# Where the first unit's low parts stand on VectorE: ahead of the folds of the phase that ends, or behind them

## The chip, the cores and the metric

The kernel runs on one core of a Trainium2 chip. The metric is the time of one execution on the device in microseconds (us), lower is better. Engines are named as the profile names them: PE is TensorE's matmul, PEld its weight load, DVE is VectorE, ACT is ScalarE, POOL is GpSimd, SP is SyncE.

## The reference

Three layers follow one another over 4 x 4096 tokens of 192 channels in float32: a causal convolution over 7 taps whose weights are a softmax for each of 8 heads, a gated layer of width 1536, and a squared-relu layer of width 2048.

```python
w = softmax(weight)                                  # [8 heads, 7 taps]
x = sum over k of w[head(c), k] * x_pad[b, s + k, c]  # 16384 x 192
gate = 1.0 / (1.0 + np.exp(-(x @ w_gate)))
x = (gate * (x @ w_val)) @ w_out                     # 192 -> 1536 -> 192
r = np.maximum(x @ w_in, 0.0)
out = (r * r) @ w_out2                               # 192 -> 2048 -> 192
```

## The kernel before

**High and low parts.** TensorE multiplies float32 in a format with fewer bits (fp32r). Every operand is therefore split into a high part (the value rounded to fp32r, written by ACT) and a low part (the value minus its high part, written by DVE), and a product is the sum of three: high x high, low x high and high x low. For the hidden activations the tiles are called `s` (the float32 value, 3 buffers), `gh` (high, 5 buffers) and `gl` (low, 5 buffers), each of 128 x 512.

**Phases and units.** The 16384 tokens are cut into 32 tiles of 512. A *phase* is one tile through one layer: kind 1 is the gated layer, kind 2 the squared-relu layer. The order is five phases of kind 1, then kind 1 and kind 2 in turn (27 of each), then the last five of kind 2: 64 phases, with 63 places where one ends and the next starts. A phase of kind 1 has 12 *units* of 128 hidden columns (one hidden tile each), a phase of kind 2 has 8 units of 256 (two hidden tiles each).

**A unit's steps.** `rows(u)` (L492) issues 18 matmuls on the PE that make the unit's two PSUM banks (`pg` and `pv`, or `ph` twice). `activate(u)` reads them: sigmoid or relu on ACT (L505), a product on DVE (`times`, L509), the high part on ACT (`high`, L514). `low` (L519) is the subtraction on DVE. `cols(u)` (L557) issues 10 matmuls for each hidden tile, which add into four PSUM banks (accA and accB, for each half of the rows). Its first two matmuls read `gh`, its next two `gl`. All these matmuls come in pairs on the two halves of 64 rows, and the two of a pair start together.

**The order of the work.** It is written out by hand; every engine works through its own queue in that order. In the main loop unit k of a phase (k from 0) does: rows(u), activate(u), then `cols` of units that are waiting, then `side[e]` (work put in by hand: a tap of the convolution, a step of the conversion of weights, a step of the preparation of the next operand), then low(u). At k = 0 both units left over from the phase that ends get their `cols`, at k = 1 none, from k = 2 on one: so the PE's order at a start is rows(u0), cols of two old units, rows(u1), rows(u2), cols(u0). When the last `cols` of a phase is issued, `fold` follows at once: ACT copies one half of the sums (L572, L576), DVE adds the other half (L573, L577), and a join (ACT L580, DVE L581) brings 64 channels together. The fold gives the four banks back; cols(u0) takes them again. In what follows u0, u1, u2 are the first three units of the phase that starts.

Of the kernel before, what the change touches and what calls it, by code (L numbers as in the profile page):

```python
# [25 lines left out]
def kernel(  # L26
# [30 lines left out]
    NU1, NU2 = F1 // P, F2 // (2 * P)  # L57
# [422 lines left out]
    def rows(u):  # L480

        xs = (x1 if u.kind == 1 else x2)[u.t]
        u.banks = [banks.take(nm) for nm in (("pg", "pv") if u.kind == 1 else ("ph", "ph"))]
        w, lo = (w1[:, u.f, :], N1 + HB) if u.kind == 1 else (weights2(u.f)[0], NR)


        place = (0, 4, 2)
        steps = [(c, o, p) for c in range(C) for o, p in ((0, 0), (0, 1), (lo, 0))]
        for i, (n, o, p) in enumerate(steps):
            for h, half in enumerate(HALVES):  # L490
                c = n ^ h if n < 2 else n
                nc.tensor.matmul(  # L492
                    u.banks[h][1], w[half, o + c * P : o + (c + 1) * P],
                    xs[1][half, place[n] + p, :],
                    start=(i == 0), stop=(i == len(steps) - 1),
                )
        if u.last:
            operands.give(xs)
# [18 lines left out]
    def low(v):  # L517
        v.gl = gp.tile([P, NT], F32R, tag="gl", name="gl", bufs=5)
        nc.vector.tensor_tensor(v.gl, v.s, v.gh.bitcast(F32), op=ALU.subtract)  # L519

    def activate(u):

        acts = []
        for i in range(1 if u.kind == 1 else 2):
            acts.append(act(u, i))
            times(u, acts[-1])
        banks.give(*u.banks)
        u.hidden = [high(s) for s in acts]
# [3 lines left out]
    def cols(u):  # L532

        key = (u.kind, u.t)
        if u.f == 0:
            acc[key] = [[banks.take(f"acc{nm}") for nm in "AB"] for _ in HALVES]
        sums = acc[key]
        order = []  # L540
        for i, v in enumerate(u.hidden):
            if u.kind == 1:
                w, lo = w1[:, u.f, NR:], N1 + HB
            else:
                w, lo = weights2(u.f)[1][:, i, :], NO + HB
            wa, wb, wl = w[:, 0:P], w[:, P : 2 * P], w[:, lo : lo + P]
            first = u.f == 0 and i == 0
            order += [
                (0, wa, v.gh, first), (0, wa, v.gl, False), (0, wl, v.gh, False),
                (1, wb, v.gh, first), (1, wb, v.gl, False),  # L550
            ]
        if u is units[-1]:
            order.sort(key=lambda step: -step[0])
        ends = {step[0]: k for k, step in enumerate(order)} if u.last else {}
        for k, (b, wt, m, first) in enumerate(order):
            for h, half in enumerate(HALVES):
                nc.tensor.matmul(  # L557
                    sums[h][b][1], wt[half], m[half], start=first, stop=ends.get(b) == k,
                )
        return u.last  # L560
# [97 lines left out]
    with tc.manual_schedule():  # L658
# [85 lines left out]
        def convert_and_activate(e, u):  # L744

            one, two = (conv[i] if i < NU1 else None for i in (e + 1, e + 2))
            if two:
                two.word()
            if one:
                one.place()  # L750
                one.follow()
                one.sign()
                if e + 1 + NRAW < NU1:
                    conv[e + 1 + NRAW].load()
            s = act(u, 0)
            if one:
                one.highs()
            if e:
                low(units[e - 1].hidden[0])
            if one:  # L760
                one.power()
                one.lows()
            if two:
                two.middle()
            times(u, s)
            banks.give(*u.banks)
            u.hidden = [high(s)]
            if 1 <= e <= K:
                a1[e]()
            if e == NU1 - 1:  # L770
                low(u.hidden[0])
            if 0 <= e - K - 1 < len(parts1):
                parts1[e - K - 1]()

        for e, u in enumerate(units):
            rows(u)
            if e < NU1:
                convert_and_activate(e, u)
            else:
                activate(u)  # L780
            for o in stores:
                o()
            stores = []
            k = e - max(s for s in starts if s <= e)
            due = len(pending) if k == 0 else 0 if k == 1 else len(pending) - 1
            for _ in range(due):
                v = pending.popleft()
                if cols(v):
                    stores += (evac1 if v.kind == 1 else evac2)(v.t)
            pending.append(u)  # L790
            for o in side[e]:
                o()
            if e >= NU1:
                for v in u.hidden:
                    low(v)
        while pending:
            v = pending.popleft()
# [42 lines left out]
```

## Time and profile before

| | |
|---|---|
| median of 3 runs | 2390.89 us (2389.89 to 2391.37) |
| the profiled execution: its own time | 2391.61 us |
| the profiled execution: span, first to last instruction | 2389.5 us |
| mean granted TensorE clock | 0.997 of full speed |
| busy: PE, DVE, ACT | 99%, 70%, 55% of the span |

The span is what the trace covers; the time of the same execution is 2.1 us longer. A start time in the trace counts from the start of the span. The end of a matmul is modelled and matmuls overlap, so the distance between starts says more on the PE than the busy time does.

### The profile page before, as it was taken

Reading aid. Unit: us, or ns where it says so; the run is one execution under the profiler, and the core shown is the slowest. Engines: PE = TensorE matmul, PEld = TensorE weight load, DVE = VectorE, ACT = ScalarE, POOL = GpSimd, SP = SyncE. Lnnn points to the kernel's source line nnn. Section 1 sums busy time; section 2 is a strip of 40 time slices with the busy share of each in tenths; the row PEclk is TensorE's granted clock in tenths of the full one; section 3 lists DMA queues with packets and bytes.
Section 4 is the critical chain, followed back from the end, with each engine's and each line's share of the span. In section 5 each row is a group of like instructions: output and inputs, shape, how many; then the busy total and the mean of one; then the engine's idle time right before and its main releaser. Section 6 shows DMA issues by size and latency. Waiting matters only on the chain.

```text
span 2389.5 us, 49288 instructions
## 1 busy us (share of the span) xinstructions
PE 2362.3 (99%) x20522; PEld 1930.7 (81%) x20522; DVE 1680.4 (70%) x2677; ACT 1315.6 (55%) x2260; POOL 46.4 (2%) x98
## 2 busy tenths in 40 slices
PE   9999999999999999999999999999999999999998
PEld 5788788888888888888888888888888888888887
DVE  7887867667666767667767677676776766766776
ACT  6556655555555555555555455554555555555665
POOL 1000000000000000000000000000000000000000
PEclk9999999999999999999999999999999999999999
DMA  6222211111112012121011210111111111101111
GB/s 156 58 54 69 51 30 39 38 26 32 30 39 43 21 32 43 25 43 35 20 41 25 43 39 21 37 39 30 39 29 29 38 30 39 34 21 28 40 28 27
DMA packets 226399, 92.12 MB, mean 39 GB/s; under 512 B 202344, under 2 KB 213744, under 8 KB 226176
## 3 DMA queue, kind: packets, MB, share of 16 engines
q1 hardware_dynamic: 224688, 88.19, 17.2%
q8 instruction: 160, 2.62, 0.5%
q0 software_dynamic: 288, 0.59, 0.1%
q14 instruction: 63, 0.52, 0.1%
q10 hardware_dynamic: 1200, 0.20, 0.0%
HBM read 26.03 MB, written 12.58 MB: 16 GB/s over the span
## 4 chain that ended last, share of the span: by engine, by line
PE 78%; issue 16%; DVE 3%; ACT 2%; DMA 1%; SPq 0%; POOLq 0%; DVEq 0%; ACTq 0%; POOL 0%
PE pg L492 28%; PE accA L557 20%; PE ph L492 14%; PE accB L557 13%; PE pv L492 1%; ACT gh L514 1%; DVE s L509 1%; ACT s L505 1%; DVE cvA L390 0%; DVE y L573 0%; DVE gl L519 0%; ACT tb L580 0%; DVE cb L577 0%; ACT ca L572 0%; DVE yb L581 0%
## 5 line engine op out<-in xcount | busy, mean ns | idle before, releaser
L492 PE MATMUL pg<-x,w 64*128 64x512 f32 x3456 | 845.0, 388 | 5.3 <-ACT w L181 3.0
L492 PE MATMUL pv<-x,w 64*128 64x512 f32 x3456 | 844.8, 388 | 0.4 <-DMA x<-x 0.4
L514 ACT CAST gh<-s 128x512 fp32r<-128x512 f32 x896 | 556.9, 623 | 439.1 <-DVE s L509 431.8
L492 PEld LDWEIGHTS pg<-x,w 64*128 64x128 f32 x3456 | 638.3, 185 | 140.0 <-ACT w L181 6.8
L557 PE MATMUL accA<-gh,w 64*128 64x512 f32 x3584 | 699.7, 387 | 0.0
L519 DVE TENSOR_TENSOR gl<-s,gh 128x512 fp32r<-128x512 f32 x896 | 598.5, 686 | 73.0 <-ACT gh L514 56.0
L492 PEld LDWEIGHTS pv<-x,w 64*128 64x128 f32 x3456 | 638.5, 185 | 5.5 <-DMA x<-x 0.9
L492 PE MATMUL ph<-x,w 64*128 64x512 f32 x4608 | 558.9, 386 | 0.0
L492 PEld LDWEIGHTS ph<-x,w 64*128 64x128 f32 x4608 | 432.3, 184 | 90.2
L509 DVE TENSOR_TENSOR s<-pv,s 128x512 f32<-128x512 f32 x384 | 264.5, 689 | 274.5 <-ACT s L505 274.2
L509 DVE TENSOR_TENSOR s<-s 128x512 f32<-128x512 f32 x512 | 330.2, 686 | 159.0 <-ACT s L505 159.0
L505 ACT ACTIVATE s<-ph 128x512 f32<-128x512 f32 x512 | 284.8, 595 | 231.3 <-PE ph L492 182.0
L557 PEld LDWEIGHTS accA<-gh,w 64*128 64x128 f32 x3584 | 337.1, 184 | 73.2 <-issue 4.5
L505 ACT ACTIVATE s<-pg 128x512 f32<-128x512 f32 x384 | 229.2, 597 | 266.4 <-PE pv L492 257.1
L557 PE MATMUL accA<-gl,w 64*128 64x512 f32 x1792 | 353.2, 390 | 12.4 <-DVE gl L519 12.2
L557 PE MATMUL accB<-gh,w 64*128 64x512 f32 x1792 | 349.9, 387 | 0.0
L557 PE MATMUL accB<-gl,w 64*128 64x512 f32 x1792 | 349.7, 387 | 0.0
L557 PEld LDWEIGHTS accA<-gl,w 64*128 64x128 f32 x1792 | 168.5, 184 | 58.7 <-DVE gl L519 25.1
L557 PEld LDWEIGHTS accB<-gl,w 64*128 64x128 f32 x1792 | 168.5, 184 | 35.3
L557 PEld LDWEIGHTS accB<-gh,w 64*128 64x128 f32 x1792 | 168.4, 184 | 35.3
L390 DVE SCALAR_TENSOR_TENSOR cvA<-xTA,cw,cvA 128x512 f32<-128x512 f32 x186 | 137.4, 739 | 0.6 <-ACT cvA L386 0.2
L573 DVE TENSOR_TENSOR ca<-accA,ca 128x512 f32<-128x512 f32 x32 | 22.1, 691 | 100.0 <-ACT ca L572 100.0
(80 smaller groups left out, 787.9 us busy)
## 6 DMA issues: line engine op xcount, KB each, us to landing
x<-x SPq DMA_DIRECT2D x192, 256.0 KB, 3.8
out_dram<-oA SPq DMA_DIRECT2D x126, 64.0 KB, 1.9
xiA<-in_x_dram SPq DMA_DIRECT2D x124, 64.0 KB, 2.8
raw<-in_moe_w_out_dram SPq DMA_DIRECT2D x28, 192.0 KB, 3.5
out_dram<-oB SPq DMA_DIRECT2D x63, 64.0 KB, 1.9
xiB<-in_x_dram SPq DMA_DIRECT2D x60, 64.0 KB, 2.3
raw<-in_moe_w_in_dram SPq DMA_DIRECT2D x16, 192.0 KB, 4.1
raw<-in_moe_w_gate_dram SPq DMA_DIRECT2D x12, 192.0 KB, 3.8
```

The source lines that it names most:

```text
L390: nc.vector.scalar_tensor_tensor(out=st["cv"], in0=st["x"][:, k : k + NT], scalar=cw[:, i, k : k + 1], in1=st["cv"], op0=ALU.mult, op1=ALU ...
L492: nc.tensor.matmul(u.banks[h][1], w[half, o + c * P : o + (c + 1) * P], xs[1][half, place[n] + p, :], start=(i == 0), stop=(i == len(steps ...
L505: nc.scalar.activation(s, u.banks[i][1], AF.Sigmoid if u.kind == 1 else AF.Relu)
L509: nc.vector.tensor_tensor(s, u.banks[1][1] if u.kind == 1 else s, s, op=ALU.mult)
L514: nc.scalar.copy(v.gh, s)
L519: nc.vector.tensor_tensor(v.gl, v.s, v.gh.bitcast(F32), op=ALU.subtract)
L557: nc.tensor.matmul(sums[h][b][1], wt[half], m[half], start=first, stop=ends.get(b) == k,)
L573: nc.vector.tensor_tensor(dst_a, a0[1], ca, op=ALU.add)
```

## The change

At k = 0 of a phase the low parts of u0 are issued before the waiting `cols` and the fold, instead of after them and after `side[e]`. At every other k, and in the very first phase, nothing changes.

```diff
             k = e - max(s for s in starts if s <= e)
+
+            if e >= NU1 and k == 0:
+                for v in u.hidden:
+                    low(v)
             due = len(pending) if k == 0 else 0 if k == 1 else len(pending) - 1
             for _ in range(due):
                 v = pending.popleft()
...
             pending.append(u)
             for o in side[e]:
                 o()
-            if e >= NU1:
+            if e >= NU1 and k:
                 for v in u.hidden:
                     low(v)
```

Only DVE's queue changes its order; the rows of the PE, of ACT, of POOL and of SP stand as they did. DVE has as many instructions as before.

First, DVE at the start of a phase of kind 2 (`s<-s` is the relu's square of u0, `y` and `yb` are what the fold of the ending phase of kind 1 writes, `cvA` is a tap of the convolution out of `side`):

```order
 L509 TENSOR_TENSOR s<-s 128x512 x2
-L573 TENSOR_TENSOR y<-accA,ca 128x512
-L577 TENSOR_TENSOR cb<-accB,cb 128x512
-L581 TENSOR_TENSOR yb<-cb,tb 64x512
-L390 SCALAR_TENSOR_TENSOR cvA<-xTA,cw,cvA 128x512
-L519 TENSOR_TENSOR gl<-s,gh 128x512 x2
+L519 TENSOR_TENSOR gl<-s,gh 128x512 x2
+L573 TENSOR_TENSOR y<-accA,ca 128x512
+L577 TENSOR_TENSOR cb<-accB,cb 128x512
+L581 TENSOR_TENSOR yb<-cb,tb 64x512
+L390 SCALAR_TENSOR_TENSOR cvA<-xTA,cw,cvA 128x512
 L509 TENSOR_TENSOR s<-s 128x512 x2
```

The two low parts move past the three instructions of the fold and past the tap. Where a phase has no `side` work at k = 0, they move past the fold alone.

Second, DVE at the start of the first phase of kind 2, where `side` also holds three steps of a conversion of weights (`cvt`, `cvq`), before the change:

```order
L509 TENSOR_TENSOR s<-s 128x512 x2
L573 TENSOR_TENSOR y<-accA,ca 128x512
L577 TENSOR_TENSOR cb<-accB,cb 128x512
L581 TENSOR_TENSOR yb<-cb,tb 64x512
L161 TENSOR_SCALAR cvt<-cvt 128x384
L167 TENSOR_SCALAR cvq<-cvq 128x384
L174 SCALAR_TENSOR_TENSOR cvt<-raw,cvt 128x384
L390 SCALAR_TENSOR_TENSOR cvA<-xTA,cw,cvA 128x512
L519 TENSOR_TENSOR gl<-s,gh 128x512 x2
L509 TENSOR_TENSOR s<-s 128x512 x2
```

In the changed kernel the `gl` row stands second, and seven instructions come after it that came ahead of it.

Third, DVE at the second phase's start, where a phase of kind 1 follows one of kind 1 and `side` holds the transposes of the next input (`xTA`, `xTB`), in the changed kernel:

```order
L509 TENSOR_TENSOR s<-pv,s 128x512
L519 TENSOR_TENSOR gl<-s,gh 128x512
L573 TENSOR_TENSOR y<-accA,ca 128x512
L577 TENSOR_TENSOR cb<-accB,cb 128x512
L581 TENSOR_TENSOR yb<-cb,tb 64x512
L377 STREAM_TRANSPOSE xTA<-xiA 128x512
L377 STREAM_TRANSPOSE xTB<-xiB 128x512
L509 TENSOR_TENSOR s<-pv,s 128x512
```

Here one low part moves past five instructions; before, it stood between the transposes and the last row.

## Rows read from the trace of the kernel before

**Rows 1.** The page: TensorE's busy time, and its granted clock in 40 slices.

```profile
PE 2362.3 (99%) x20522; PEld 1930.7 (81%) x20522; DVE 1680.4 (70%) x2677; ACT 1315.6 (55%) x2260; POOL 46.4 (2%) x98
...
PEclk9999999999999999999999999999999999999999
```

**Rows 2.** Waits, whole span: who waited for whom, us in total, times, longest.

```profile
PEld accA L557 <- DVE gl L519: 25.1, 32, 2.1
...
PE accA L557 <- DVE gl L519: 12.2, 16, 1.7
```

**Rows 3.** Busy time by windows: between two starts of cols(u0), length first.

```profile
647.02:717.29 70.27, 70.27 (x622) 58.15 (x620) 49.79 (x78) 38.19 (x66) 1.63 (x3) 1.00 0.16 33
```

**Rows 4.** Line L557 over the span: the last start of its matmuls.

```profile
L557 PE MATMUL accA<-gh,w x3584: 383/386/497, 35.3 to 2381.5; 64*128 64x512 f32 x200
```

**Rows 5.** Timeline, PE: a kind-2 start with a tap; start, us, instruction, idle before.

```profile
717.29 0.39 PE L557 MATMUL accA<-gh,w 64*128 64x512 f32 x2
718.39 0.50 PE L557 MATMUL accA<-gl,w 64*128 64x512 f32 x2 [0.71 <-DVE gl L519]
718.73 0.40 PE L557 MATMUL accA<-gh,w 64*128 64x512 f32 x2
...
720.58 1.75 PE L492 MATMUL ph<-x,w 64*128 64x512 f32 x14
```

**Rows 6.** Timeline, DVE, same start.

```profile
714.31 0.69 DVE L573 TENSOR_TENSOR y<-accA,ca 128x512 f32<-128x512 f32 x1 [1.17 <-ACT ca L572]
...
716.28 0.69 DVE L581 TENSOR_TENSOR yb<-cb,tb 64x512 f32<-64x512 f32 x1 [0.69 <-ACT tb L580]
716.98 0.75 DVE L390 SCALAR_TENSOR_TENSOR cvA<-xTA,cw,cvA 128x512 f32<-128x512 f32 x1
717.65 1.29 DVE L519 TENSOR_TENSOR gl<-s,gh 128x512 fp32r<-128x512 f32 x2
...
720.23 1.30 DVE L519 TENSOR_TENSOR gl<-s,gh 128x512 fp32r<-128x512 f32 x2
```

**Rows 7.** Timeline, ACT, same start.

```profile
712.56 1.23 ACT L514 CAST gh<-s 128x512 fp32r<-128x512 f32 x2 [0.27 <-DVE s L509]
713.69 0.58 ACT L572 COPY ca<-accA 128x512 f32<-128x512 f32 x1
```

**Rows 8.** Timeline, PE: a kind-2 start without a tap.

```profile
644.49 0.39 PE L557 MATMUL accA<-gh,w 64*128 64x512 f32 x2
...
647.02 2.21 PE L492 MATMUL ph<-x,w 64*128 64x512 f32 x18
```

**Rows 9.** Timeline, PE: the first start of kind 2.

```profile
277.30 0.39 PE L557 MATMUL accA<-gh,w 64*128 64x512 f32 x2
279.40 0.50 PE L557 MATMUL accA<-gl,w 64*128 64x512 f32 x2 [1.71 <-DVE gl L519]
...
281.58 2.20 PE L492 MATMUL ph<-x,w 64*128 64x512 f32 x18
```

**Rows 10.** Timeline, PE and DVE, second phase: cols(u0), then u2's low part and its use.

```profile
83.12 0.39 PE L557 MATMUL accA<-gh,w 64*128 64x512 f32 x2
84.03 0.50 PE L557 MATMUL accA<-gl,w 64*128 64x512 f32 x2 [0.52 <-DVE gl L519]
...
89.22 0.69 DVE L519 TENSOR_TENSOR gl<-s,gh 128x512 fp32r<-128x512 f32 x1
...
90.53 0.39 PE L557 MATMUL accA<-gl,w 64*128 64x512 f32 x2
```

**Rows 11.** Timeline, PE and DVE, fourth phase: u3's low part and its use.

```profile
170.19 0.69 DVE L519 TENSOR_TENSOR gl<-s,gh 128x512 fp32r<-128x512 f32 x1
...
171.21 0.39 PE L557 MATMUL accA<-gl,w 64*128 64x512 f32 x2
```

**Rows 12.** Timeline, DVE and PE: a start of kind 1 after kind 2.

```profile
678.09 0.68 DVE L519 TENSOR_TENSOR gl<-s,gh 128x512 fp32r<-128x512 f32 x1
...
679.44 0.39 PE L557 MATMUL accA<-gl,w 64*128 64x512 f32 x2
```

## The prediction, on record before the changed kernel was run

> **What bounds the kernel now.** I read the page first. The PE is busy in 2362.3 of 2389.5 us, and its granted clock shows a 9 in all 40 slices [rows 1], so the clock needs no term. The kernel can only become faster where the PE waits. The second view is the list of waits: the one large wait of the PE and its weight load, after the start-up, is on `gl` from L519, the very instruction that the change moves: 32 waits of the weight load (25.1 us) and 16 of the matmul (12.2 us) [rows 2]. These two overlap, so neither is the loss. I took the loss from starts instead.
>
> A window without such a wait gives the pace. From 647.02 to 717.29 the PE is busy for all 70.27 us [rows 3]. In it the program issues 310 pairs of matmuls: what is left of a kind-2 phase after three rows (5 rows of 9 pairs, 7 cols of 20 halves, that is 70 pairs, so 115), a kind-1 phase (12 x 14 = 168) and three rows of the next (27). 70.27 / 310 = 0.2267 us a pair. The whole kernel has 32 x (12 x 28 + 8 x 38) = 20480 such matmuls, 10240 pairs. When cols(u0) of the second phase starts at 83.12, 168 + 27 = 195 of them are behind it; the 10044 steps from there to the last start at this pace take 2276.8 us and would end at 2359.9. The last start is at 2381.5 [rows 4]. So **21.6 us** are lost between 83 us and the end. If all of it is stalls of this one kind, 21.6 us is also the most that the change can bring.
>
> It is. I went through the PE's timeline at all 63 starts. In 32 of them, those at which the phase that ends is of kind 1, cols(u0) is held up: its two matmuls on `gh` start, its first pair on `gl` waits. In the other 31 nothing is held up.
>
> - Starts of kind 2 with one tap in `side` (12 of them): cols(u0) starts at 717.29 and the next rows at 720.58, 3.29 us for 20 halves that need 10 x 0.2267 = 2.27 [rows 5]. Loss 1.02, together 12.2. The `gl` pair starts 1.10 after the pair ahead, and the pair behind it still takes 0.34, so a stall costs some 0.15 more than its wait.
> - Starts of kind 2 without a tap (13): 647.02 - 644.49 - 2.27 = 0.26 [rows 8], together 3.4.
> - The first start of kind 2, with a conversion of weights and a tap: 281.58 - 277.30 - 2.27 = 2.0 [rows 9]. The last one loses 0.3.
> - The five starts of kind 1 after kind 1: 0.4 to 1.1 each, 3.7 together; the first of them waits from 83.12 to 84.03 where 0.23 is needed [rows 10].
>
> 12.2 + 3.4 + 2.0 + 0.3 + 3.7 = 21.6, which is the loss found from the pace.
>
> Of the size of this loss the two ways to read the PE disagree: by its idle time only 12.2 us hang on `gl` [rows 2]; by starts it is 21.6. The Trainium skill (Perfetto Trace Analysis, Identifying the Most-Contended Engine) says that matmul busy time is a bad measure because pipelined matmuls overlap in the record. By idle time alone the change would bring 12 us and end near 2379; by starts 21 us. The trace sides with starts: where they show a gap of 1.10, the record shows 0.71 idle [rows 5].
>
> **Why `gl` is late.** DVE works in order. At the start with a tap, it waits 1.17 us for ACT's `ca`, adds `y` at 714.31, comes to the join at 716.28, to the tap at 716.98, and only then, at 717.65, to the two low parts of u0 [rows 6]. Their inputs were there long before: ACT wrote both `gh` from 712.56 to 713.79, ahead of `ca` [rows 7]. The first matmul of cols(u0) at 717.29 went through, so the banks that the fold gives back were already free; what was late is `gl` alone.
>
> **The change, part by part.**
> (1) The low parts at their new place. They can start when the first `gh` is done, about 713.2 (half of 1.23 after 712.56). A run of two takes 1.29, and DVE is free for the next after about 1.2, since neighbours overlap. The second must wait for 713.79, so DVE is free at about 714.45. The idle 1.17 before `y` covers all of it but some 0.15 to 0.2. `gl` is then ready near 714.5, 3 us before the PE wants it at 717.29 + 0.23. The loss goes: 1.02 at each of the 12, and the same reckoning holds for the 15 others of kind 2 (5.7 together).
> (2) The fold starts up to 0.2 later. Costed at nothing: its first sum ends near 715.2 instead of 715.0, the second 0.6 later, and the banks are wanted from 717.29 on: 2.1 us of cover remain for the first and 1.5 for the second. Without this cover the price would be 0.2 at each of the 63 starts, 13 us.
> (3) What is late next: u1. DVE reaches u1's product after fold and tap, now without the 1.2 us of low parts ahead of it but with a fold 0.2 later, so 1.0 us sooner. u1's first low part, at 720.23 before [rows 6], comes near 719.2, ready by 720.0. The PE wants it 2.04 + 0.23 after 720.58 less the 1.02, at 721.8. Fine. At the first start of kind 2 the same steps leave only about 0.2 us, still no wait.
> (4) The early starts of kind 1 are tighter, since DVE also does transposes, two taps or a conversion there, and ACT sits in that chain. In the second phase u2's low part runs from 89.22 to 89.91 and is used at 90.53 [rows 10]. Here u1's product waited for ACT and the transposes, not for the low part, so nothing moves forward; with the fold 0.1 later the low part ends at 90.0. The PE comes 0.83 sooner (0.91 less 0.23, and the tail of 0.15), at 89.7: a new stall of 0.35, with its tail 0.5. In the fourth phase u3's low part ends at 170.88 and is used at 171.21 [rows 11], a slack of 0.33; DVE gains about 0.5 there, the PE its loss of 0.9: a stall of 0.2, with its tail 0.3. In the sixth u1 has a like shortfall of 0.1, with tail 0.25. I give back 1.0 of the 3.7. The bounds: 0 (DVE's order gives more than I count) and all of 3.7 plus the first kind-2 start's 2.0.
> (5) The 31 starts at which kind 2 ends: no loss before, since four hidden tiles of cols give the fold time: `gl` at 678.09 is ready 0.68 before its use at 679.44 [rows 12]. They gain nothing and have nothing to lose; in five of them, kind 2 after kind 2, a low part must now also wait for an old `gl` buffer, which the PE has read through some 1.1 us after rows(u0), before `gh` is there.
>
> The sum: 21.6 - 1.0 = 20.6. The profiled execution took 2391.61 us, so 2371.0; the median of before lies 0.7 below that execution, and so I put the new one at **2370.3**.
>
> **Rivals.**
> A, *the stall moves to u1 and u2 in part*: speaks for it that slack after u0 is thin in the early phases [rows 10, 11]; against it, in the 25 regular starts u1 has almost 2 us [rows 6]. If the six irregular starts give back all of their 5.7, 16 us remain: 2375.
> B, *the change does nothing, since the wait on L519 stands for another*: the fold's banks, with the PE held until the fold's end. Then the first pair of cols(u0), which writes the same banks, would wait too; it does not [rows 5]. Time 2391.
> C, *slower: a low part that waits for `gh` blocks the fold behind it*, the banks come late, and cols(u0) waits from its first pair. That costs nothing up to 2.1 us of delay; beyond that, each us costs 1 us at each of 32 starts, and to lose more than the 21.6 gained the delay must exceed 2.1 + 0.7. A delay of 4 us would make it 2391 + 32 x 1.2 = 2429. Against it: ACT writes `gh` ahead of `ca`, for which the fold waits anyway [rows 7], so the delay can't exceed the low parts' own 1.2. The Trainium skill (TensorE: Matmul & The Clock Gate, the table at its head, engine queue depth) calls VectorE's queue a strict FIFO of eight, which speaks for C; by that rule alone the fold is held as long as `gh` is missing, which the trace puts at zero beyond `ca`.
>
> **How the numbers follow.** The forecast, 19.5 to 21.6 saved, has 0.80; A 0.13; B 0.04; C 0.02; 0.01 for what I don't see. A difference under 0.2% (4.8 us) can't be told from none. Faster 0.93, same 0.04, slower 0.03. The range: all 21.6 from the fastest run of before (2389.89) gives 2368 at the low end, A's 2375 the high one; between them lie the forecast and most of A.
>
> **What the new profile should show.** The waits of PE and PEld on `gl` shrink from 32 to a few, in the second, fourth and sixth phase, under 0.5 us each. At kind-2 starts cols(u0) takes 2.27 us, DVE's idle before `y` falls from 1.17 to near 0, and `y` comes up to 0.2 later relative to the PE. The span ends near 2369. Wrong if cols(u0)'s first pair waits (C), if u1's `gl` is waited for in the regular starts (A), or if the pace of 0.2267 a pair changes.

## The result

The changed kernel takes 2370.63 us (median of 4 runs, 2369.92 to 2372.77) against 2391.13 us (4 runs): ratio 0.9916, 95% interval 0.9904 to 0.9927. The forecast was 2370.3, in a range of 2368 to 2375. The profiled execution took 2370.91 us, with a span of 2369.1 us at a granted clock of 0.997.

The waits of the PE and its weight load in the changed kernel (who waited for whom, us in total, times, longest). Of the two lines of [rows 2] the PE's is gone, and the weight load's is down to one wait of 0.2 us. What else is left belongs to the start-up, apart from two short waits on `s`:

```profile
PEld pg L492 <- ACT w L181: 7.1, 6, 2.1
...
PE pg L492 <- ACT w L181: 3.2, 4, 1.2
PE pg L492 <- DMA x<-x: 1.8, 1, 1.8
...
PEld pv L492 <- DVE s L509: 0.8, 2, 0.5
...
PEld accA L557 <- DVE gl L519: 0.2, 1, 0.2
```

The PE's timeline at the kind-2 start that [rows 5] show before (start, length in us):

```profile
710.05 0.47 PE L557 MATMUL accA<-gh,w 64*128 64x512 f32 x2
710.27 0.47 PE L557 MATMUL accA<-gl,w 64*128 64x512 f32 x2
...
712.31 1.07 PE L492 MATMUL ph<-x,w 64*128 64x512 f32 x7
```

cols(u0) takes 2.26 us, where it took 3.29; the `gl` pair follows the pair on `gh` by 0.22 instead of 1.10. DVE at the same start, to be held against [rows 6]:

```profile
705.97 1.29 DVE L519 TENSOR_TENSOR gl<-s,gh 128x512 fp32r<-128x512 f32 x2
707.18 0.68 DVE L573 TENSOR_TENSOR y<-accA,ca 128x512 f32<-128x512 f32 x1
707.78 0.68 DVE L577 TENSOR_TENSOR cb<-accB,cb 128x512 f32<-128x512 f32 x1
709.14 0.69 DVE L581 TENSOR_TENSOR yb<-cb,tb 64x512 f32<-64x512 f32 x1 [0.68 <-ACT tb L580]
709.85 0.75 DVE L390 SCALAR_TENSOR_TENSOR cvA<-xTA,cw,cvA 128x512 f32<-128x512 f32 x1
710.52 1.28 DVE L509 TENSOR_TENSOR s<-s 128x512 f32<-128x512 f32 x2
```

The two low parts fill the idle 1.17 us that stood before `y`; `y` has no wait any more. Against cols(u0) it comes 2.87 us ahead, 2.98 before: the fold is 0.11 later, and nothing waits for it.

The loss can be taken as in the prediction: from the start of cols(u0) of the second phase to the last start, less 2276.8 us. The timeline gives the one end, the row of line L557 (durations, then first and last start) the other:

```profile
83.16 0.42 PE L557 MATMUL accA<-gh,w 64*128 64x512 f32 x2
```

```profile
L557 PE MATMUL accA<-gh,w x3584: 385/386/497, 35.4 to 2361.2; 64*128 64x512 f32 x200
```

2361.2 - 83.16 - 2276.8 = 1.2 us, where 21.6 were lost before and 1.0 was expected. This figure, good to about 0.1 us, is used for every kernel below, since it leaves out the start-up, whose end moves between 82.3 and 84.5 us from one profiled execution to the next.

### The profile page after: what moved, and what is told of

Read it like the earlier page. It is cut to its first block, busy times and chain, and to the rows that moved or that the text cites. A ratio compares the mean times of both kernels' runs of the same rounds, so it can differ in the third digit from the quotient of the medians.

```text
span 2369.1 us, 49298 instructions
## 1 busy us (share of the span) xinstructions
PE 2353.5 (99%) x20522; PEld 2306.8 (97%) x20522; DVE 1687.0 (71%) x2677; ACT 1313.4 (55%) x2260; POOL 45.7 (2%) x98
## 4 chain that ended last, share of the span: by engine, by line
PE 83%; issue 15%; DMA 1%; DVE 0%; ACT 0%; SPq 0%; POOLq 0%; DVEq 0%; ACTq 0%; POOL 0%
PE accA L557 21%; PE pg L492 18%; PE ph L492 17%; PE accB L557 14%; PE pv L492 13%; DMA x<-x 0%; DMA raw<-in_moe_w_out_dram 0%; PE cv L399 0%; SPq L144 0%; ACT s L505 0%; DVE s L509 0%; SPq L332 0%; ACT w L181 0%; DVE gl L519 0%; ACT gh L514 0%
## 5 line engine op out<-in xcount | busy, mean ns | idle before, releaser
L557 PE MATMUL accA<-gh,w 64*128 64x512 f32 x3584 | 827.9, 386 | 0.0
L492 PEld LDWEIGHTS ph<-x,w 64*128 64x128 f32 x4608 | 531.3, 184 | 0.0
L557 PEld LDWEIGHTS accA<-gh,w 64*128 64x128 f32 x3584 | 480.9, 184 | 7.8 <-issue 4.6
L557 PE MATMUL accA<-gl,w 64*128 64x512 f32 x1792 | 422.6, 386 | 0.0
L557 PE MATMUL accB<-gh,w 64*128 64x512 f32 x1792 | 422.4, 386 | 0.0
L557 PE MATMUL accB<-gl,w 64*128 64x512 f32 x1792 | 422.3, 386 | 0.0
L557 PEld LDWEIGHTS accB<-gh,w 64*128 64x128 f32 x1792 | 240.4, 184 | 1.7
L557 PEld LDWEIGHTS accB<-gl,w 64*128 64x128 f32 x1792 | 240.4, 184 | 1.7
L557 PEld LDWEIGHTS accA<-gl,w 64*128 64x128 f32 x1792 | 240.2, 184 | 1.7 <-DVE gl L519 0.2
L580 ACT COPY tb<-cb 64x512 f32<-64x512 f32 x64 | 39.5, 618 | 59.0 <-DVE cb L577 59.0
```

What stands on the lines that cost most here:

```text
L492: nc.tensor.matmul(u.banks[h][1], w[half, o + c * P : o + (c + 1) * P], xs[1][half, place[n] + p, :], start=(i == 0), stop=(i == len(steps ...
L557: nc.tensor.matmul(sums[h][b][1], wt[half], m[half], start=first, stop=ends.get(b) == k,)
L580: nc.scalar.copy(tb[HALVES[own]], cb[HALVES[1 - own]])
```

## The experiments

The kernel before, on the same chips, had medians of 2390.81 (21 runs, beside the first four) and 2390.99 (15 runs, beside the others). Edits are shown against the changed kernel, but for the one on the ring of `s`; `...` stands for lines left out.

| | median us | ratio, 95% interval | loss after the start-up, us |
|---|---|---|---|
| low parts between fold and side | 2381.80 | 0.9961 (0.9947 to 0.9974) | 11.2 |
| kind-2 starts alone | 2373.48 | 0.9926 (0.9914 to 0.9939) | 3.7 |
| kind-1 starts alone | 2388.19 | 0.9990 (0.9981 to 0.9999) | 18.9 |
| order of before, 4 buffers for `s` | 2391.06 | 1.0002 (0.9993 to 1.0010) | 21.7 |
| changed, 2 more subtractions | 2371.89 | 0.9920 (0.9906 to 0.9934) | 2.5 |
| changed, 6 more subtractions | 2442.74 | 1.0214 (1.0200 to 1.0228) | 73.9 |
| changed, side work later | 2372.12 | 0.9920 (0.9907 to 0.9934) | 1.9 |
| starts after kind 2 alone | 2390.65 | 1.0000 (0.9991 to 1.0008) | 21.3 |

**Half of the way: behind the fold, ahead of side.**

```diff
-            if e >= NU1 and k == 0:
-                for v in u.hidden:
-                    low(v)
             due = len(pending) if k == 0 else 0 if k == 1 else len(pending) - 1
...
             pending.append(u)
+            if e >= NU1 and k == 0:
+                for v in u.hidden:
+                    low(v)
             for o in side[e]:
                 o()
             if e >= NU1 and k:
```

> The low parts of u0 stand behind the fold but ahead of side at k = 0. By my reading only the time at which gl is ready counts. At the 12 kind-2 starts with a tap gl comes 0.67 us sooner than before the change, so a stall of some 0.35 us each is left of 1.02 (8.0 gained); the 13 without a tap keep their 0.26; the first kind-2 start gains about 1, the early kind-1 starts together about 1.8, since u1 and u2 become late in their turn. Sum 10.9: about 2380 us, with 25 or more waits on gl left. Rival 1, that only the side work in front mattered and the fold did not: all of the gain, 2370.6. Rival 2, that only the place ahead of the fold mattered: no gain, 2391.

Measured: 2381.80 us, 11.2 us of loss left (10.7 expected), 29 waits of the weight load on `gl`. At a start with a tap, in the timelines of DVE and the PE, by time:

```profile
714.84 1.29 DVE L519 TENSOR_TENSOR gl<-s,gh 128x512 fp32r<-128x512 f32 x2
...
715.59 0.50 PE L557 MATMUL accA<-gl,w 64*128 64x512 f32 x2
...
716.05 0.74 DVE L390 SCALAR_TENSOR_TENSOR cvA<-xTA,cw,cvA 128x512 f32<-128x512 f32 x1
```

The PE's pair starts 0.75 after DVE's low part, at whatever place that part stands (before: 718.39 against 717.65 [rows 5, 6]). The fold, with its waits for ACT, and the side work both held the low part back; neither rival stands, and about half of the gain came from either. One part of the sum was too high: taken from one cols(u0) to the next, the early phases of kind 1 still lose 2.8 of 3.7 us, so they gained 0.9 and not 1.8.

**The parts of the sum.** The change at the 27 kind-2 starts alone, and at the five starts of kind 1 after kind 1 alone:

```diff
-            if e >= NU1 and k == 0:
+            first = e >= NU1 and k == 0 and u.kind == 2 and units[e - 1].kind == 1
+            if first:
...
-            if e >= NU1 and k:
+            if e >= NU1 and not first:
```

> The change at the 27 starts of kind 2 alone. By the sum of the prediction 12.2 + 3.4 + 2.0 + 0.3 = 17.9 us gained: 2373.2. If the stalls are not worth what their gaps say (idle time alone, about half): 2381.

> The change at the five starts of kind 1 after kind 1 alone. Gain 3.7 less what comes back as new stalls (1.2 in the changed kernel): 2.5 us, 2388.6. With the other part alone it should add up to the whole change. If the parts do not add up, one of them also acts on the other's starts.

Measured: 17.3 us gained by the first (17.9 expected), 2.6 by the second (2.5). In the loss after the start-up the first leaves 3.7, the sum of the five kind-1 stalls to the tenth; the second leaves 18.9. Together 17.9 + 2.7 = 20.6 of loss removed, and the whole change removed 20.4: the parts add up.

**The starts at which nothing waited.** The same two lines, with `units[e - 1].kind == 2` as the condition.

> The change only at the 31 starts where a phase of kind 2 ends, at which the PE waited for nothing before. No gain and no loss: 2391.

Measured: 2390.65 us, ratio 1.0000. The 31 starts give nothing, and the low part ahead of the fold costs nothing there either.

**The ring of `s`.** The kernel before, with its order; `idle` is a tile of the start-up out of the same ring:

```diff
-        s = gp.tile([P, NT], F32, tag="s", name="s")
+        s = gp.tile([P, NT], F32, tag="s", name="s", bufs=4)
...
-        idle = gp.tile([P, NT], F32, tag="s", name="idle")
+        idle = gp.tile([P, NT], F32, tag="s", name="idle", bufs=4)
```

> The kernel before the change, order untouched, with a fourth buffer for s. In the kernel before, ACT waits 46.7 us for an s buffer that a late low part still reads, and the change takes most of that wait away. My theory: the PE waits for gl itself, which does not come sooner, so no gain: 2391, with 32 waits of PEld on gl as before and ACT's wait for s gone. Rival: the ring of s is what holds the chain, and the gain can be had by the buffer alone: well below 2385.

Measured: 2391.06 us. Its list of waits:

```profile
PEld accA L557 <- DVE gl L519: 25.3, 32, 2.1
...
PE accA L557 <- DVE gl L519: 12.4, 17, 1.7
```

ACT's wait for `s`, 46.7 us before, is gone from the list, and the PE waits as it did. The change also removes most of that wait (5.9 us are left), but as a by-product that brings no time: the rival falls.

**How late the fold may be.** The changed kernel, in which each low part of u0 is written n more times at the 27 kind-2 starts:

```diff
             if e >= NU1 and k == 0:
                 for v in u.hidden:
                     low(v)
+                    if u.kind == 2 and units[e - 1].kind == 1:
+                        for _ in range(n):
+                            nc.vector.tensor_tensor(
+                                v.gl, v.s, v.gh.bitcast(F32), op=ALU.subtract
+                            )
```

> The changed kernel with two more subtractions on DVE ahead of the fold at each of the 27 kind-2 starts (each low part is written once more), 1.2 us in front of the fold. In the changed kernel the fold's first sum ends 2.2 us before cols(u0) wants its banks, so 1.2 us should cost nothing at 26 starts and about 1.0 us at the first one, where u1 has 0.3 us of slack: 2371.6. If a fold that is held costs from its first microsecond on: 27 x 1.2 = 32, so 2403.

> The same with six more subtractions, 3.6 us ahead of the fold. That is 1.4 us over the cover of 2.2, plus a tail of 0.15: 1.57 x 26 = 41, some 0.1 each at the starts with a tap where u1 is then late too, and some 3 at the first: about 2416, with the first pair of cols(u0) waiting for the fold's sums. Rival, that the DVE's idle time later in the phase absorbs a late fold: within 10 us of 2371. Rival, that every microsecond counts: 27 x 3.6 = 97, so 2468.

Measured with n = 1: 2371.89 us, loss 2.5 against 1.2. The fold is held 1.45 us longer at 27 starts (four subtractions take 2.66 from first start to first start of `y`, where two take 1.21), and together that costs 1.3 us, all at the first of them, where the PE waits for u1's `gl`:

```profile
280.49 0.50 PE L557 MATMUL accA<-gl,w 64*128 64x512 f32 x2 [0.92 <-DVE gl L519]
```

With n = 3: 2442.74 us, 27 us above the figure expected. Timeline of DVE and of the PE at one start:

```profile
723.61 0.69 DVE L519 TENSOR_TENSOR gl<-s,gh 128x512 fp32r<-128x512 f32 x1
724.33 2.15 DVE L791 TENSOR_TENSOR gl<-s,gh 128x512 fp32r<-128x512 f32 x3
726.39 0.68 DVE L519 TENSOR_TENSOR gl<-s,gh 128x512 fp32r<-128x512 f32 x1
727.11 2.15 DVE L791 TENSOR_TENSOR gl<-s,gh 128x512 fp32r<-128x512 f32 x3
729.18 0.68 DVE L573 TENSOR_TENSOR y<-accA,ca 128x512 f32<-128x512 f32 x1
...
723.60 4.26 PE L492 MATMUL ph<-x,w 64*128 64x512 f32 x36
729.91 0.50 PE L557 MATMUL accA<-gh,w 64*128 64x512 f32 x2 [2.05 <-DVE y L573]
...
732.34 2.29 PE L492 MATMUL ph<-x,w 64*128 64x512 f32 x18
...
736.81 2.20 PE L492 MATMUL ph<-x,w 64*128 64x512 f32 x18
```

Eight subtractions take 5.57 us from the first start to `y`, where two took 1.21 in the changed kernel: the fold is held 4.4 us, not the 3.6 that I had put in. A subtraction that writes the same tile again follows at 0.72 (723.61, 724.33), while the two low parts of the changed kernel, which write two tiles, follow at 0.60 (1.21 for both). With 4.4 the reckoning holds: 4.4 - 2.2 of cover = 2.2 of wait. Rows end at 727.68 (723.60 + 18 x 0.2267), cols(u0) starts at 729.91, 2.23 later. From 727.68 to the next rows at 732.34 it is 2.39 more than the 2.27 needed; cols(u1) ends 4.47 later, 0.16 more than 4.31. So this start, one with a tap, loses 2.55. Taken in the same way at all 27, ten starts with a tap lose 2.55 to 2.57, thirteen without one, where u1 is less late, 2.35 to 2.42, and the first 4.3. Three more lose 3.9 to 4.0, though their wait before cols(u0) is no longer. There the clock fell: from 0.6 us after the start of cols(u0) at 353.40 (and from its very start at 1029.91 and 2081.31) pairs follow at 0.43 instead of 0.23, for about 3 us. The timeline of the PE, and the busy times of that stretch (length, PE, PEld, DVE, ACT, POOL; then the granted clock):

```profile
353.40 0.50 PE L557 MATMUL accA<-gh,w 64*128 64x512 f32 x2 [2.08 <-DVE y L573]
...
355.12 0.63 PE L557 MATMUL accA<-gh,w 64*128 64x512 f32 x2
355.55 0.63 PE L557 MATMUL accA<-gl,w 64*128 64x512 f32 x2
...
354.10:357.30 3.20, 3.20 (x20) 2.50 (x18) 2.60 (x5) 2.82 (x6) 0.00 (x0) 0.50 0.02 5
```

This is the lower of TensorE's two levels, 1.2 of 2.4 GHz, right after the PE had stood idle for 2.08 us; why it came at these three and not at the other 24 the runs don't show. All 27 together lose 72.5 of the 72.7 us added. And it is the first pair that waits now, on `y`:

```profile
PEld accA L557 <- DVE y L573: 67.1, 27, 2.5
PE accA L557 <- DVE y L573: 55.7, 27, 2.1
```

This is the prediction's rival C, brought about by the padding: it exists, it costs next to nothing below its cover, and at the one delay beyond it that was tried the PE waits for all that exceeds the cover.

**The last microsecond.** In the changed kernel, at k = 0 the side work is kept back and done at k = 1, after u1's low part:

```diff
             pending.append(u)
+            if e >= NU1 and k == 0:
+                later = side[e]
+                continue
+            if e >= NU1 and k == 1:
+                for v in u.hidden:
+                    low(v)
+                for o in later:
+                    o()
             for o in side[e]:
                 o()
-            if e >= NU1 and k:
+            if e >= NU1 and k > 1:
                 for v in u.hidden:
                     low(v)
```

> The changed kernel with the side work of k = 0 done after the low parts of u1, ahead of the side work of k = 1. It aims at the 1.2 us that are still lost in the second, fourth and sixth phase, where u1's product stands behind transposes, taps or a conversion. My theory: they go but for some 0.2, and nothing else moves: a span about 1 us shorter, 2369.6. Rival: the work only comes later, u2 and u3 have little slack there, and the stalls move on to them: 2371 or more.

Measured: 2372.12 us, 1.5 us over the changed kernel's median; the intervals overlap. Its start-up was 1.3 us longer in the profiled run, with a longer wait on a DMA that the edit does not touch; but the loss after it is 1.9 against 1.2 too: the second, fourth and sixth phase lose 0.6 each, where the changed kernel loses 0.7, 0.3 and 0.3. In the timelines cols(u0) of the second phase starts at 84.47, and in the sixth phase the PE waits one unit later than in the changed kernel:

```profile
84.47 0.39 PE L557 MATMUL accA<-gh,w 64*128 64x512 f32 x2
...
241.65 0.74 DVE L390 SCALAR_TENSOR_TENSOR cvA<-xTA,cw,cvA 128x512 f32<-128x512 f32 x1
242.31 0.68 DVE L509 TENSOR_TENSOR s<-pv,s 128x512 f32<-128x512 f32 x1
...
243.05 0.49 PE L492 MATMUL pv<-x,w 64*128 64x512 f32 x1 [0.33 <-DVE s L509]
```

Its wait in the start-up:

```profile
PE pg L492 <- DMA x<-x: 4.7, 1, 4.7
```

In the sixth phase u2's product now stands behind the conversion and the tap, and rows(u4) waits for the bank that it reads. The rival was right: the side work has to go somewhere in these phases, and the stall goes with it. No kernel here is better than the changed one.

## Why the prediction was right, point by point

- **The loss and its places.** 21.6 us in 32 starts. The parts removed one by one give 17.9 and 2.7 of it, the 31 other starts give none. Of the two ways to size it, starts were right: the PE's idle time on `gl`, 12.2 us [rows 2], would have had the kernel end at 2379, outside what was measured. The Trainium skill (Perfetto Trace Analysis, Identifying the Most-Contended Engine) says that matmul busy share is not a good measure of how close a kernel is to its roofline. This case agrees: the share only rose from 98.9 to 99.3% of the span while 20 us went.
- **(1) `gl` at its new place**: right. Both parts are ready at 707.26, the first of them 3.6 us before the PE's pair, and the stall is gone at all 27 kind-2 starts.
- **(2) The fold 0.2 later, costed at nothing**: right in kind and size. It is 0.11 later; the cover of 2.1 us, which the prediction only argued, was measured by the padded kernels: 1.45 us of delay is free but for the first start, 4.4 costs 2.2 and its tail.
- **(3) u1 in the regular starts**: right, no wait. At the first kind-2 start too.
- **(4) The early phases**: right in sum (1.2 given back, 1.0 forecast), and right in mechanism in the fourth (0.3 for 0.3, at u3's `gl`). In the second the step failed: I had put the new stall at u2's `gl` in cols(u2), and it stands a unit earlier, at rows(u3). In the sixth (0.3 for 0.25) it failed in part: some of the stall is at rows(u3), the rest at cols(u1). The timelines of DVE and the PE in the changed kernel, second phase:

```profile
84.30 0.69 DVE L509 TENSOR_TENSOR s<-pv,s 128x512 f32<-128x512 f32 x1 [0.74 <-ACT s L505]
...
84.32 0.49 PE L492 MATMUL pg<-x,w 64*128 64x512 f32 x1
85.05 0.50 PE L492 MATMUL pv<-x,w 64*128 64x512 f32 x1 [0.23 <-DVE s L509]
...
87.00 0.61 PE L557 MATMUL accA<-gh,w 64*128 64x512 f32 x2
```

  rows(u3) writes the banks that u1 used, and `pv` is only free when u1's product has read it, at 84.99; the rows that need 2.04 us take from 84.32 to 87.00, 0.64 more. I had followed `gl` from unit to unit and the banks only through the fold. That the cost came out near (0.64 for 0.5) is in part luck: u1's late product stands ahead of u2's low part in DVE's queue too, but the wait that cost the time was never reckoned.
- **(5) The 31 starts after kind 2**: right, 1.0000.
- **The rivals.** A (later units) is the 1.2 us, no more. B fell already in the trace of before, and with the change. C is real, but lies behind 2.2 us of cover, of which the change uses 0.1. What no reckoning here had is the clock, which fell at three of the waits of 2 us in the kernel with six more subtractions.

## What to carry to other kernels

When the busiest engine waits for an instruction whose inputs were ready long ago, look at what stands ahead of it in its own in-order queue; an idle gap there, in which that queue waits for something else, took the instruction for free here. Before moving it, reckon what it delays by the length of the idle gap and the slack of what comes behind it, and check the next unit's buffers as well as its data. Size a stall on the PE by the distance between starts, including the slow pair after it, not by the idle time that the record shows.

## What was not expected of the hardware

The weight load's busy share rose from 81% [rows 1] to 97% in the changed kernel, with the same 20522 loads of the same length. Windows of the changed kernel (length, then busy time of PE, PEld, DVE, ACT, POOL):

```profile
647.00:717.00 70.00, 70.00 (x621) 70.00 (x619) 51.43 (x80) 36.80 (x64) 1.63 (x3) 1.00 0.16 33
```

PEld is busy all of the time here, and was for 58.15 of 70.27 us in [rows 3], at the same pace. The cause is in the starts. The timeline of the changed kernel in a phase of kind 1:

```profile
680.58 0.39 PE L492 MATMUL pg<-x,w 64*128 64x512 f32 x1
680.66 0.39 PE L492 MATMUL pv<-x,w 64*128 64x512 f32 x1
680.81 0.39 PE L492 MATMUL pg<-x,w 64*128 64x512 f32 x1
680.89 0.39 PE L492 MATMUL pv<-x,w 64*128 64x512 f32 x1
```

The two halves start 0.08 and 0.14 us apart in turn; in the kernel before they start together. The offset arises in the early phases of the changed kernel, whose short stalls hold one half longer than the other, and stays to the end, since no later stall brings the halves together again (with two more subtractions the stall at 280.49 does). Their loads then lie side by side instead of on top of each other. The kernel with the kind-2 starts alone has no offset and PEld at 57.86 of the same 70 us, and as its loss is the one expected, the offset neither costs nor gains time that these runs can show:

```profile
647.00:717.00 70.00, 70.00 (x620) 57.86 (x618) 49.80 (x78) 37.13 (x65) 1.63 (x3) 1.00 0.16 33
```
